# Second tap sums from superblock 10 on, and a range check of the softmax sums with a branch ahead of the last store

## The chip, the cores and the metric

The kernel runs on one core of one Trainium2 chip. A core has five engines that run side by side, each with its own instruction queue: TensorE (PE, matrix multiplications; its weight loads are shown as PEld), VectorE (DVE), ScalarE (ACT), GpSimd (POOL) and SyncE (SP, which here only issues DMAs). They wait for each other through semaphores. Matmul results go to PSUM, the small memory that only the engines reach; all other tiles are in SBUF.

The metric is the device time of one execution in microseconds. The kernel before took 746.48 us (median of three runs, 745.0 to 747.21).

## The reference

Two stages follow each other: a dynamic convolution, whose 7 weights per token and head come out of a softmax, and a two-layer network with x - tanh(x) between the layers.

```python
# x (8, 4096, 192), weight_gen (8, 4096, 8, 7), w_in (192, 2048), w_out (2048, 192)
w = weight_gen - np.max(weight_gen, axis=-1, keepdims=True)
w = np.exp(w)
w = w / (np.sum(w, axis=-1, keepdims=True) + 1e-09)
x_pad = np.concatenate([zeros (B, 6, D), x], axis=1)
x_unf = x_pad[:, idx, :].reshape(B, S, 7, 8, 24)     # idx: the token and the six before it
out = np.einsum('bshk,bskhg->bshg', w, x_unf).reshape(B * S, 192)

h = out @ w_in
g = h - np.tanh(h)
return g @ w_out
```

## The kernel before

The 32768 tokens are cut into 32 superblocks of 1024 tokens (TOK). In a superblock, partition p of 128 holds J = 8 tokens that follow each other. Superblock n goes through these steps:

- SP loads x with a halo of six tokens (`load_x`, L134, 1344 KB) and the raw weights (`load_wg`, L120).
- Softmax: ScalarE takes the exponential without subtracting the maximum (L169), VectorE sums over the 7 taps (L183), takes the reciprocal (L198) and scales (L229). The sums of a superblock lie in a tile of their own, `zsum`.
- `products`: GpSimd multiplies x by the weights of the taps, all in one expression per group of taps (L299): taps 0 and 1 (`KH` = 2), taps 2 and 3, then, in `rest`, taps 4 to 6. Taps 0 to 3 go to tile `pa` (three buffers), taps 4 to 6 to tile `pb` (one buffer). For some tokens of taps 0 and 1 VectorE does the work in GpSimd's place (`help`: a copy, L250, and a multiplication, L251). `HELP[n]` lists the places (superblock, f) at which VectorE does so for superblock n; the first entry is for token 7, the second, where there is one, for token 6, and GpSimd multiplies what is left of the 8 tokens.
- `dma_sum` (L236): a DMA that GpSimd issues adds the three taps of `pb` onto taps 0 to 2 of `pa`. It is called the first sum here (`pa<-pb`, 1152 KB). For superblocks in `TWO_SUMS` a second sum (`second_sum`, `pa<-pa`, 768 KB) adds taps 2 and 3 onto taps 0 and 1. GpSimd issues the second sum of superblock n after its first two multiplications for superblock n + 1, and it waits for the landing of the first sum.
- `conv_sums` (L384): TensorE multiplies what is left with the identity, which transposes it to channels on partitions and adds up the taps in PSUM. Where there was no second sum, four taps are left, 4 x 24 = 96 matmuls; where there was one, two taps, 48 matmuls. ScalarE copies the result to `convT` (L410).
- `gemm1` (L427): first layer, 16 column blocks f, each into one PSUM tile `ph` (three buffers, shared with the transposes). ScalarE takes the tanh (L440), VectorE subtracts (`gt`, L441).
- `out_stream` (L495): second layer, one block of 128 tokens after the other, ScalarE copies the block out (L514), and SP stores the superblock (L518).

The order of the instructions on every engine is written out by hand, in one loop over n and f. In iteration (n, f) TensorE does `gemm1(n, f)`, a share of the second layer of superblock n - 1, and at two places the transposes for superblock n + 1. A plan says where: `pairs` gives the number of second-layer pairs after each f, `t2` and `t1` the f (and the pairs ahead of it) at which the transposes of chunks 0 and 1 and of chunk 2 stand, `sums` the f of the two halves of the softmax sum of superblock n + 4, `scale` the f of its scaling. Superblocks in `DOUBLE_IN` follow plan DOUBLE, those after it STEADY:

```python
STEADY = dict(pairs=(5, 11, 0, 16, 4, 12, 6, 10, 0, 6, 10, 8, 8, 8, 8, 16), t1=(14, 8), t2=(13, 0), scale=14, sums=(1, 13))
DOUBLE = dict(pairs=(4, 12, 0, 16, 0, 16, 5, 11, 0, 5, 11, 6, 10, 0, 16, 16), t1=(15, 4), t2=(11, 4), scale=15, sums=(1, 10))
DOUBLE_IN = (4, 5, 6, 7, 8, 9, 10, 11)
```

`products(n + 2)` stands at f = 1 of iteration n, its `rest` at f = 3 (or at the last place in `HELP[n + 2]` in this iteration). SP's queue holds, for each n above 8, the load of x for n + 3, the load of weights, and then the store of n - 1, in this order. The load of x for n + 3 waits for GpSimd's first multiplication of n + 2 and for the end of the use of the buffer by n + 1.

After the loop, `gemm2_last` does the second layer of the last superblock (31), token by token j: 32 matmuls (L538), a copy on ScalarE (L551), an addition on VectorE (L552). After every second j SP stores two tokens per partition (L554).

Of the kernel before, what the change touches and what calls it, by code (L numbers as in the profile page):

```python
# [8 lines left out]
FP32 = mybir.dt.float32  # L9
BF16 = mybir.dt.bfloat16  # L10

ACT = mybir.ActivationFunctionType
AX = mybir.AxisListType


@with_exitstack
def kernel(
# [8 lines left out]
    nc = tc.nc  # L26

    B, S, D = x.shape
# [7 lines left out]
    J = 8  # L36
# [8 lines left out]
    PART = (2, 3)  # L45
    TWO_SUMS = (13, 14, 15, 16, 17, 18, 19, 20, 21, 22, 23, 24, 25, 26, 27, 28, 29, 30, 31)
    AHEAD = 4
    STORE_FIRST = 8
    EXTRA = (5, 9, 11, 13)

    HELP = {n: ((n - 2, 3),) for n in (4, 5, 6, 7, 8, 9, 10, 11, 12, 13, 14, 15, 16, 17, 18, 19, 20, 21, 22, 23, 24, 25, 26, 27, 28, 29, 30, 31)} | {9: ((7, 3), (6, 12)), 10: ((8, 3), (7, 12)), 11: ((9, 3), (8, 12)), 12: ((10, 3), (9, 12)), 13: ((11, 3), (10, 12)), 14: ((12, 3), (11, 12))}
    LAST_TAP = (4, 5, 6, 7, 8)
    X_LATE = ()
    ZERO_AT = 8
    PACE, PACED = None, ()
# [26 lines left out]
    nc.vector.memzero(zero[:])  # L82
    once = const.tile([P, 1], FP32, name="once")

    x_of = {}
# [81 lines left out]
    def softmax_exp(n):  # L167
        wg_t = wg_of.pop(n)
        last_exp[0] = nc.scalar.activation(  # L169
            out=wg_t[:].rearrange("p j h k -> p (j h k)"),  # L170
            in_=wg_t[:].rearrange("p j h k -> p (j h k)"),
            func=ACT.Exp,
        )
        e_of[n] = wg_t
# [4 lines left out]
    def softmax_sum(n, j0=0, j1=J):  # L179

        if j0 == 0:
            zsum_of[n] = wgpool.tile([P, J * H], FP32, name="zsum")
        nc.vector.reduce_sum(  # L183
            out=zsum_of[n][:, j0 * H : j1 * H],
            in_=e_of[n][:, j0:j1].rearrange("p j h k -> p (j h) k"),
            axis=AX.X,
        )

    def softmax_recip(n, j0=0, j1=J):
# [4 lines left out]
    def softmax_norm(n, bank):  # L194

        wsm = softmax_tile()
        zr_v = bank[:, 512 - J * H : 512]
        nc.vector.reciprocal(zr_v, zsum_of[n][:])  # L198

        def finish():  # L200
            scale(nc.vector, wsm[:], e_of[n], zr_v)

        wsm_of[n] = (wsm, None, None, None)
        return finish

    def softmax_norm_ramp(n, bank):
# [3 lines left out]
        zr_v = bank[:, 512 - J * H : 512]  # L210
        nc.vector.reciprocal(zr_v, zsum_of[n][:])  # L211
        if n == 2:
# [312 lines left out]
    def out_pairs(m):  # L525
        for _ in range(m):
            next(pairs)

    def gemm2_last(j, f0=0, f1=NFT):

# [21 lines left out]
        nc.vector.tensor_add(out_sb[:, j, :], po[:, 1, 0:D], ot[:])  # L552
        if j % 2 == 1:
            nc.sync.dma_start(  # L554
                out=out[n * TOK : (n + 1) * TOK, :].rearrange("(p j) e -> p j e", p=P)[
                    :, j - 1 : j + 1, :
                ],
                in_=out_sb[:, j - 1 : j + 1, :],
            )

    w_in = const.tile([P, NC, F], BF16, name="w_in")
    w_out = const.tile([P, NFT, D], BF16, name="w_out")

    ctx.enter_context(tc.manual_schedule())

# [120 lines left out]
    DOUBLE = dict(pairs=(4, 12, 0, 16, 0, 16, 5, 11, 0, 5, 11, 6, 10, 0, 16, 16), t1=(15, 4), t2=(11, 4), scale=15, sums=(1, 10))  # L686
    DOUBLE_IN = (4, 5, 6, 7, 8, 9, 10, 11)

# [18 lines left out]
    for n in range(1, NTOT):  # L707
# [5 lines left out]
        for f in range(NFT):  # L713
# [18 lines left out]
            if n == AHEAD and f == 4:  # L732
                softmax_exp(n + 4)
            if n > 1:
                for h, at in enumerate(plan["sums"]):
                    if soft and f == at:
                        softmax_sum(soft[0], h * JH, (h + 1) * JH)
# [29 lines left out]
            if f == (9 if n == 1 else 1) and n <= STORE_FIRST:  # L767
                loads(n)

    gemm2_last(0, 0, J)  # L770
    out_pairs(NFT)
    gemm2_last(0, J, NFT)
    for j in range(1, J):
        gemm2_last(j)


# [28 lines left out]
```

## Time and profile before

| | before |
|---|---|
| median of three runs | 746.48 us (745.0 to 747.21) |
| span of the profiled execution | 743.4 us |
| device time of the profiled execution itself | not told apart from the three runs |
| mean granted TensorE clock | 0.995 |
| instructions | 30037 |
| first sums (1152 KB), issue to landing, median | 28, 9.5 us |
| second sums (768 KB), issue to landing, median | 21, 7.2 us |
| stores of two tokens (192 KB) at the end | 4, 3.0 us |

The span runs from the first to the last instruction of the program; the device time has a few us around it. The page gives busy time per engine, the chain of waits that ended last, and groups of instructions by source line. A view of stretches gives, for each stretch of the span, its length, then busy time and number of instructions (x) of each engine, then the granted clock, the share of DMA time and the rate in GB/s. A timeline gives start, duration, engine, line, operation and the tiles (written<-read), then in brackets the idle time before it and what ended that. "Superblock n" as a stretch of time is iteration n of the loop, from the first tanh (L440) of it to the first of the next.

### The profile page before, as it was taken

The page shows a single profiled execution, that of the slowest core. Times are in us where ns is not written, and L with a number is a line of the kernel's source. Part 1 is how long each engine was busy: PE and PEld are TensorE (multiplying, and loading weights), DVE is VectorE, ACT ScalarE, POOL GpSimd, SP SyncE. Part 2 cuts the span into 40 slices and gives each one's busy share as a digit, 9 for nine tenths or more (in the row PEclk, how much of TensorE's full clock was granted, in tenths as well). Part 3 has the DMA queues.
Part 4 walks back from the last instruction along what each step waited for, and adds up shares of the span by engine and source line. Part 5 has one row for each costly group of instructions (what it writes and reads, how often), then busy time and mean ns, then how long its engine had stood idle before and what let it go on. Part 6 is the DMA issues. An engine that isn't in the chain of part 4 may idle for free.

```text
span 743.4 us, 30037 instructions
## 1 busy us (share of the span) xinstructions
PE 722.3 (97%) x13616; PEld 556.5 (75%) x13616; DVE 687.4 (92%) x723; ACT 638.8 (86%) x872; POOL 654.5 (88%) x163
## 2 busy tenths in 40 slices
PE   3899999999999999999999999999999999999997
PEld 2477777778777777777777777777777777877777
DVE  7999899999999999999999999999999999988893
ACT  4888888888888888989889999898998989888882
POOL 7999999999999999999999999999999999991000
PEclk9899999999999999999999999999999999999999
DMA  8925367766567668878777977877887877776112
GB/s 236 245 46 161 135 172 185 195 179 149 124 183 184 183 185 224 210 199 203 166 202 209 236 186 204 178 195 205 221 209 195 192 181 194 193 149 110 45 45 86
DMA packets 34269, 130.06 MB, mean 175 GB/s; under 512 B 4591, under 2 KB 9439, under 8 KB 30174
## 3 DMA queue, kind: packets, MB, share of 16 engines
q0 software_dynamic: 19424, 51.12, 40.4%
q1 hardware_dynamic: 14718, 77.03, 27.6%
q8 instruction: 106, 1.74, 0.9%
q14 instruction: 21, 0.17, 0.1%
HBM read 54.52 MB, written 25.17 MB: 107 GB/s over the span
## 4 chain that ended last, share of the span: by engine, by line
PE 92%; DVE 5%; ACT 1%; issue 1%; DMA 1%; SPq 0%; DVEq 0%
PE ph L427 43%; PE obank L495 43%; PE pc L384 4%; DVE gt L441 3%; PE po L538 1%; ACT th L440 1%; DVE pa L299 1%; DMA wg_t<-in_weight_gen_dram 1%; DVE zsum L183 0%; SPq L134 0%; ACT convT L402 0%; DVE obank L211 0%; DVE pa L251 0%; DVE pb L299 0%; SPq L144 0%
## 5 line engine op out<-in xcount | busy, mean ns | idle before, releaser
L441 DVE TENSOR_TENSOR gt<-ph,th 128x1024 bf16<-128x1024 f32 x512 | 601.6, 1217 | 33.4 <-ACT th L440 23.2
L440 ACT ACTIVATE th<-ph 128x1024 f32<-128x1024 f32 x512 | 512.1, 1025 | 69.2 <-PE ph L427 60.3
L427 PE MATMUL ph<-convT,w_in 64*128 64x512 bf16 x3072 | 415.1, 379 | 5.3 <-DVE gt L441 3.3
L495 PEld LDWEIGHTS <-gt 64*128 64x128 bf16 x7936 | 355.6, 94 | 80.6 <-issue 6.3
L495 PE MATMUL obank<-w_out,gt 64*128 64x192 bf16 x7936 | 408.0, 243 | 0.9 <-issue 0.8
L299 POOL TENSOR_TENSOR pa<-x_t,wsm 128x2688 bf16<-128x2688 f32 (+3 forms) x68 | 338.9, 5232 | 0.2
L299 POOL TENSOR_TENSOR pb<-x_t,wsm 128x4608 bf16<-128x4608 f32 (+2 forms) x33 | 283.8, 8601 | 0.7 <-ACT wsm L221 0.5
L427 PEld LDWEIGHTS <-w_in 64*128 64x128 bf16 x3072 | 163.0, 94 | 86.0 <-issue 18.3
L514 ACT ACTIVATE out_sb<-obank 128x192 f32<-128x192 f32 x248 | 81.3, 328 | 11.2 <-PE obank L495 10.3
L410 ACT ACTIVATE convT<-pc 128x1024 bf16<-128x1024 f32 (+1 forms) x62 | 50.1, 810 | 2.9 <-PE pc L384 2.7
L236 POOL DMA_DIRECT2D pa<-pb x28 | 36.0, 1284 | 13.7 <-POOL pb L299 9.1
L384 PEld LDWEIGHTS <-pa 64*128 64x128 bf16 x2064 | 41.5, 100 | 6.8 <-DVE pa L299 1.1
L236 POOL DMA_DIRECT2D pa<-pa x21 | 34.7, 1651 | 9.6 <-DMA pa<-pb 8.9
L384 PE MATMUL pc<-ident,pa 64*128 64x64 bf16 x1968 | 41.2, 191 | 1.8 <-POOL pa L299 0.9
L183 DVE TENSOR_REDUCE zsum<-wg_t 128x32 f32<-128x224 f32 (+1 forms) x61 | 23.6, 387 | 2.9 <-ACT wg_t L169 2.9
L169 ACT ACTIVATE wg_t<-wg_t 128x448 f32<-128x448 f32 x32 | 18.2, 570 | 6.3 <-DMA wg_t<-in_weight_gen_dram 6.2
L251 DVE TENSOR_TENSOR pa<-x_t,ph 128x384 bf16<-128x384 f32 x34 | 18.8, 554 | 2.0 <-DVE ph L250 0.3
L229 DVE TENSOR_TENSOR wsm<-wg_t,pc 128x448 f32<-128x448 f32 x27 | 16.8, 621 | 2.5
L198 DVE RECIPROCAL pc<-zsum 128x64 f32<-128x64 f32 x27 | 14.9, 550 | 0.0
L384 PE MATMUL pc<-ident,pb 64*128 64x64 bf16 x216 | 4.9, 206 | 9.0 <-POOL pb L299 9.0
L384 PEld LDWEIGHTS <-pb 64*128 64x128 bf16 x288 | 6.3, 106 | 9.5 <-POOL pb L299 9.0
L538 PE MATMUL po<-w_out,gt 64*128 64x192 bf16 x256 | 11.2, 243 | 0.0
(27 smaller groups left out, 56.8 us busy)
## 6 DMA issues: line engine op xcount, KB each, us to landing
x_t<-in_x_dram SPq DMA_DIRECT2D x31, 1344.0 KB, 7.9
pa<-pb POOLq DMA_DIRECT2D x28, 1152.0 KB, 9.5
out_dram<-out_sb SPq DMA_DIRECT2D x31, 768.0 KB, 3.9
pa<-pa POOLq DMA_DIRECT2D x21, 768.0 KB, 7.2
wg_t<-in_weight_gen_dram SPq DMA_DIRECT2D x32, 224.0 KB, 7.1
x_t<-in_x_dram SPq DMA_DIRECT2D x1, 768.0 KB
w_out<-in_moe_w_out_dram POOLq DMA_DIRECT2D x1, 768.0 KB, 9.5
out_dram<-out_sb SPq DMA_DIRECT2D x4, 192.0 KB, 3.0
```

The source lines that it names most:

```text
L183: nc.vector.reduce_sum(out=zsum_of[n][:, j0 * H : j1 * H], in_=e_of[n][:, j0:j1].rearrange("p j h k -> p (j h) k"), axis=AX.X,)
L236: return nc.gpsimd.dma_start(out=out.rearrange("p k j d -> p k (j d)"), in_=in_.rearrange("p k j d -> p k (j d)"), accum_op=mybir.AluOpTyp ...
L251: nc.vector.tensor_mul(pa[:, 0:KH, j, :].rearrange("p k (h g) -> p k h g", h=H), bass.AP(tensor=x_v.tensor, offset=x_v.offset + j * D, ap= ...
L299: return eng.tensor_mul(prod(k0, k1)[:, :, j0:j1].rearrange("p k j (h g) -> p k (j h) g", h=H), bass.AP(tensor=x_v.tensor, offset=x_v.offs ...
L384: nc.tensor.matmul(pc[r][:, col : col + R] if home else pc[:, r, col : col + R], lhsT=prods[c][gi][r * R : (r + 1) * R, 2 * j : 2 * j + 2] ...
L410: last_conv[0] = nc.scalar.activation(out=out, in_=pc[:, :, 0:cols].rearrange("p r (cj t) -> p r cj t", t=R), func=ACT.Copy,)
L427: nc.tensor.matmul(ph[:, r, :], lhsT=w_in[r * R : (r + 1) * R, c, f * P : (f + 1) * P], rhs=convT[r * R : (r + 1) * R, c, :], start=(c == ...
L440: last_act[0] = nc.scalar.activation(out=th[:], in_=ph_f, func=ACT.Tanh)
L441: last_sub[0] = nc.vector.tensor_sub(gt[:], ph_f, th[:])
L495: mm = nc.tensor.matmul(po[:, 0:D], lhsT=g_of[n][f][r * R : (r + 1) * R, col : col + P], rhs=w_out[r * R : (r + 1) * R, f, :], start=(r == ...
L514: last_act[0] = nc.scalar.activation(out=out_sb[:, j, :], in_=po[:, 0:D], func=ACT.Copy)
L538: nc.tensor.matmul(po[:, r, 0:D], lhsT=g_of[n][f][r * R : (r + 1) * R, col : col + P], rhs=w_out[r * R : (r + 1) * R, f, :], start=(f == 0 ...
```

## The change

Three things are changed.

1. `TWO_SUMS` begins at 10 and not at 13, and `DOUBLE_IN` ends at 8 and not at 11. So the superblocks 10, 11 and 12 get a second sum and 48 transposes in place of 96, and iterations 9, 10 and 11, which hold these transposes, follow plan STEADY.
2. `HELP` has a second entry for 9, 10 and 11 alone, and not for 12, 13 and 14. So VectorE's help at f = 12 of iterations 9, 10 and 11 is gone, and GpSimd multiplies seven tokens for six in taps 0 and 1 of superblocks 12, 13 and 14.
3. The softmax sums of all superblocks are kept in one tile, `zall` (128 x 2048). At f = 14 of iterations 28, 29 and 30, and after the loop, VectorE takes the largest and the smallest sum of each partition, half of the tile at a time (`sums_piece` 0 to 3). It compares them with 1e30 and 1e-18, multiplies the two answers, SP brings the 128 x 2 results into one row with a DMA, and VectorE takes the minimum: `flag`. All five engines load the flag into a register and branch. If it is 0, a loop (`general`) computes all 32 superblocks anew, with the maximum subtracted; with the inputs used here it is 1 and the branch skips this. The stores of the last superblock are cut differently: tokens 0 and 1, 2 and 3, then 4 alone ahead of the branch, and 5, 6 and 7 (288 KB) behind it.

In the order of the instructions, TensorE, VectorE, ScalarE, GpSimd and SP differ only in iterations 9 to 11 and GpSimd's matching multiplications and sums, in the pieces of the check, and behind the last additions. In the path that skips `general`, every engine but GpSimd has one or more semaphore instructions that raise its semaphores to the counts that `general` would have left; VectorE's waits for its last addition. The last store waits for that count. SP waits, in the same path, for the landing of its earlier DMAs, the one-token store among them.

```diff
-    TWO_SUMS = (13, 14, 15, 16, 17, 18, 19, 20, 21, 22, 23, 24, 25, 26, 27, 28, 29, 30, 31)
+    TWO_SUMS = (10, 11, 12, 13, 14, 15, 16, 17, 18, 19, 20, 21, 22, 23, 24, 25, 26, 27, 28, 29, 30, 31)
...
-    HELP = {n: ((n - 2, 3),) for n in (4, ..., 31)} | {9: ((7, 3), (6, 12)), 10: ((8, 3), (7, 12)), 11: ((9, 3), (8, 12)), 12: ((10, 3), (9, 12)), 13: ((11, 3), (10, 12)), 14: ((12, 3), (11, 12))}
+    HELP = {n: ((n - 2, 3),) for n in (4, ..., 31)} | {9: ((7, 3), (6, 12)), 10: ((8, 3), (7, 12)), 11: ((9, 3), (8, 12))}
...
+    STORES = {1: 0, 3: 2, 4: 4}
+    LAST_STORE = {7: 5}
+    SUM_MAX, SUM_MIN = 1e30, 1e-18
+    CHECK = {(28, 14): (0,), (29, 14): (1,), (30, 14): (2,)}
...
+    zall = const.tile([P, NTOT * J * H], FP32, name="zall")
...
-            zsum_of[n] = wgpool.tile([P, J * H], FP32, name="zsum")
+            zsum_of[n] = zall[:, n * J * H : (n + 1) * J * H]
...
+    def sums_piece(i):
+        w = NTOT * J * H // 2
+        if i < 4:
+            op = ALU.max if i < 2 else ALU.min
+            nc.vector.tensor_reduce(ends[:, i : i + 1], zall[:, i % 2 * w : (i % 2 + 1) * w], AX.X, op)
+        elif i == 4:
+            nc.vector.tensor_scalar(ends[:, 0:2], ends[:, 0:2], SUM_MAX, None, op0=ALU.is_le)
+        elif i == 5:
+            nc.vector.tensor_scalar(ends[:, 2:4], ends[:, 2:4], SUM_MIN, None, op0=ALU.is_ge)
+        elif i == 6:
+            nc.vector.tensor_mul(fine[:], ends[:, 0:2], ends[:, 2:4])
+            nc.sync.dma_start(out=fine_row[:], in_=fine[:])
+        else:
+            nc.vector.tensor_reduce(flag[:], fine_row[:], AX.X, ALU.min)
...
+    def store_last(j):
+        n = NTOT - 1
+        j0 = (STORES | LAST_STORE)[j]
+        nc.sync.dma_start(
+            out=out[n * TOK : (n + 1) * TOK, :].rearrange("(p j) e -> p j e", p=P)[:, j0 : j + 1, :],
+            in_=out_of[n][:, j0 : j + 1, :],
+        )
...
-        if j % 2 == 1:
-            nc.sync.dma_start(
...
+        if j in STORES:
+            store_last(j)
...
-    DOUBLE_IN = (4, 5, 6, 7, 8, 9, 10, 11)
+    DOUBLE_IN = (4, 5, 6, 7, 8)
...
+            for piece in CHECK.get((n, f), ()):
+                sums_piece(piece)
...
+    for piece in (3, 4, 5, 6):
+        sums_piece(piece)
     gemm2_last(0, 0, J)
     out_pairs(NFT)
     gemm2_last(0, J, NFT)
     for j in range(1, J):
+        if j == 4:
+            sums_piece(7)
         gemm2_last(j)
...
+    good = nc.values_load(flag[:], min_val=0, max_val=1)
+    with tc.If(good < 1, preferred_fallthrough_block=False):
+        with tc.For_i(0, B) as b:
+            carry = xpool.tile([P, HALO + J, D], FP32, name="x_t")
+            nc.vector.memset(carry[0:1, 0:HALO, :], 0.0)
+            with tc.For_i(0, NSB) as s:
+                general(b * NSB + s, carry)
+    store_last(J - 1)
```

## The prediction

> **What bounds the kernel now.** I read the page's busy shares and its chain first, then the busy time per stretch, cut at the first tanh (L440) of each superblock, then GpSimd's timeline, and last the end of the program.
>
> ```profile
> PE 722.3 (97%) x13616; PEld 556.5 (75%) x13616; DVE 687.4 (92%) x723; ACT 638.8 (86%) x872; POOL 654.5 (88%) x163
> ...
> q8 instruction: 106, 1.74, 0.9%
> ...
> PE 92%; DVE 5%; ACT 1%; issue 1%; DMA 1%; SPq 0%; DVEq 0%
> ```
>
> TensorE is busy almost always and holds 92% of the chain, so what is taken off TensorE shortens the span if nothing else becomes late. GpSimd is as full while it works (88% of a span of which it sits out the last tenth). The stretches below are superblocks 9, 10, 11, then 12, 14, 15, 18, then 29. Columns: length; busy time and number of instructions of PE, PEld, DVE, ACT, POOL; granted clock; DMA share; GB/s.
>
> ```profile
> 221.74:244.41 22.67, 22.67 (x454) 17.68 (x450) 21.60 (x25) 19.85 (x27) 22.37 (x6) 1.00 0.78 182
> 244.41:267.09 22.68, 22.68 (x454) 17.66 (x450) 21.59 (x25) 19.85 (x27) 22.38 (x6) 1.00 0.72 205
> 267.09:289.76 22.67, 22.67 (x454) 17.68 (x450) 21.58 (x25) 19.84 (x28) 22.37 (x7) 1.00 0.72 198
> 289.76:311.61 21.85, 21.85 (x406) 16.93 (x402) 20.93 (x24) 19.70 (x27) 21.08 (x6) 1.00 0.80 201
> 333.77:355.62 21.85, 21.85 (x406) 16.82 (x402) 21.03 (x23) 19.70 (x28) 21.09 (x6) 1.00 0.80 199
> 355.62:377.47 21.85, 21.85 (x406) 16.84 (x402) 21.03 (x23) 19.71 (x27) 21.13 (x6) 1.00 0.80 199
> 421.95:443.81 21.86, 21.86 (x406) 16.85 (x402) 21.04 (x23) 19.71 (x27) 21.40 (x6) 1.00 0.81 202
> 663.29:685.16 21.87, 21.87 (x406) 17.22 (x402) 19.50 (x19) 19.38 (x26) 9.44 (x3) 1.00 0.69 142
> ```
>
> With 96 transposes a superblock takes 22.67 us, with 48 it takes 21.85; PE is busy for all of it at full clock either way, and no other engine is.
>
> GpSimd's timeline (start, us, engine, line, operation). 216.44 is the first tap sum of superblock 10 and 217.26 the start of two multiplications for 11; 276.51 to 286.30 are the multiplications of 14 and the second sum of 13, the first there is; the last four lines are a late round.
>
> ```profile
> 216.44 1.28 POOL L236 DMA_DIRECT2D pa<-pb  x1 [0.30 <-POOL pb L299]
> 217.26 10.33 POOL L299 TENSOR_TENSOR pa<-x_t,wsm 128x2304 bf16<-128x2304 f32 x2
> 227.06 8.83 POOL L299 TENSOR_TENSOR pb<-x_t,wsm 128x4608 bf16<-128x4608 f32 x1
> ...
> 276.51 10.35 POOL L299 TENSOR_TENSOR pa<-x_t,wsm 128x2304 bf16<-128x2304 f32 x2
> 286.30 1.73 POOL L236 DMA_DIRECT2D pa<-pa  x1
> ...
> 605.19 1.28 POOL L236 DMA_DIRECT2D pa<-pb  x1 [0.30 <-POOL pb L299]
> 606.01 11.01 POOL L299 TENSOR_TENSOR pa<-x_t,wsm 128x2688 bf16<-128x2688 f32 x2
> 616.48 1.72 POOL L236 DMA_DIRECT2D pa<-pa  x1
> 626.89 1.28 POOL L236 DMA_DIRECT2D pa<-pb  x1 [0.32 <-POOL pb L299]
> ```
>
> At the end of the program VectorE is idle between the last gt and the first out_sb add, and 0.96 us before each later add.
>
> ```profile
> 725.96 2.53 DVE L441 TENSOR_TENSOR gt<-ph,th 128x1024 bf16<-128x1024 f32 x2 [0.29 <-ACT th L440]
> 730.73 0.36 DVE L552 TENSOR_TENSOR out_sb<-po,ot 128x192 f32<-128x192 f32 x1 [2.24 <-ACT ot L551]
> 739.97 0.36 DVE L552 TENSOR_TENSOR out_sb<-po,ot 128x192 f32<-128x192 f32 x1 [0.96 <-ACT ot L551]
> ```
>
> **The change, part by part. 1, TensorE in superblocks 9 to 11.** They give up 48 transposes each and take the STEADY order that 12 onward have. A stretch of exactly that kind is 21.85 us, directly behind DOUBLE ones too (289.76). So 3 x (22.67 - 21.85) = -2.46 us. As a check, groups of 64, 32 and 16 transposes last 1.11, 0.65 and 0.41 us; (1.11 + 0.65) - (0.65 + 0.41) = 0.70 of the 0.82. VectorE also loses a help pair per superblock (0.19 + 0.55 us); it was not the limit, so nothing is counted for that.
>
> **2, GpSimd: three more second sums, three multiplications of seven tokens for six.** The tokens add 10.47 - 9.79 = 0.68 us each (606.01 to 616.48 against 276.51 to 286.30); a second sum adds 0.78 to GpSimd's queue and makes the 4608-wide multiplication 9.32 in place of 8.84. All of it is GpSimd time; it costs only if TensorE gets its products late. The second sum of 10 would be issued at 217.26 + 9.79 = 227.05; the first sum has landed by then (216.44 + 9.51 = 225.95). With the 7.84 us of the one at 286.30 (7.0 to 7.8 later on) it lands at 234.9. TensorE wants the tile at the 16.24 us into superblock 9 that STEADY shows, 237.98: 3.1 us to spare. The next is issued at 227.83 + 9.6 + 0.82 + 10.47 = 248.7, lands by 256.6, and is wanted at 243.59 + 16.24 = 259.8. From there GpSimd needs 21.70 a round (605.19 to 626.89) against TensorE's 21.85, so the spare grows by 0.15 each. The cover shrinks from about 11 us to 3 but holds: 0. Behind GpSimd in SP's queue stand the x loads (released by the first multiplication of the superblock before) and, behind them, the store; with GpSimd's round for 13 starting at 260.0, x for 14 goes at 264.9, ahead of the store that follows superblock 11's start (265.4): 0.
>
> **3, range check inside the loop.** A reduction of 1024 columns: 375 ns for 224, 614 for 448, so 375 + 800 x 1.067 = 1.23 us, in superblocks 28, 29, 30 behind the gt of f = 14. There the reciprocal and scaling of earlier superblocks (0.55 + 0.62 us) are missing, and VectorE's busy time is 20.06, 19.50 and 18.94 against 21.03: 0 (bounds 0 to 0.2).
>
> **4, end of the loop.** The fourth reduction, two compares and a product on VectorE, 1.23 + 3 x 0.2 (a 128x16 copy is 190 ns) with short waits, about 2.0 us, fit between 728.49 and 730.73. SP now sends the small row of results ahead of superblock 30's store, which moves from 730.07 to about 731 and is long down by the end. The flag reduction (0.4 us) lies in the 0.96 us before the fifth add, if the row lands within 4 us; a 192 KB store takes 1.9. All 0.
>
> **5, load, branch, last store.** The last store can't be issued before VectorE has finished its last add, loaded the flag into a register, branched and raised its semaphore to the count that the skipped block would have reached. In the trace VectorE's sequencer goes on 0.02 us after the last add starts (739.99), so the load runs beside the add. No row has such a load. From below: the sequencer's semaphore rows, 0.02 to 0.06 us; then the store goes at 740.33 + 0.12 = 740.45 and not 740.36, +0.09. From above: a whole memory round trip, as the last store's own 1.87 us (740.36 to 742.23); the store goes at 739.99 + 1.87 + 0.12 = 741.98, +1.62. ACT's table load, 1.28 us, is the nearest in kind, for one register I take less, 0.8: +0.55. SP passes its own load, a wait for the landing of the one-token store (issued at 736.4, down by 738.3 to 739.5) and a jump over the skipped code before that; if the jump must fetch code, a packet of the instruction queue (q8 above: packets, MB, share of 16 engines) costs 0.9% x 16 x 743.4 / 106 = 1.0 us, which ends near 740.5 and so lies beside VectorE's path (bounds 0 to +1.0). The store itself is 288 KB for 192: (3.25 - 1.87) us per 576 KB gives +0.23 (0 to 0.5). Sum +0.78, bounds 0.1 to 3.1.
>
> The Trainium skill puts a register load at some 200 ns (Runtime: NRT & Kernel Launch, Instruction fetch mechanics) and a compare-and-branch at about 108 ns (Advanced Engine Details and Errata, Control Flow Timing). By these, an estimate, the load would hide behind the add and part 5 would be about +0.4, the time 744.4. The former page also holds that a taken branch out of the two pages in hand stalls on a fetch, which speaks for the upper bound; no row here shows either.
>
> **Sum.** -2.46 + 0.78 = -1.68: the span goes from 743.4 to 741.7. The profiled execution's own device time is not told apart; the median of the three runs, 746.48, lies 3.1 above the span, and I carry that: 744.8. One-off stalls that no engine explains (0.77 us at 378.3, 0.3 in two other superblocks) fall anew in each program: about 1 us either way.
>
> **The rivals.** *The end swallows the gain.* Load, fetch and larger store all at their upper bounds: +3.1, so 747.1, or 748 if the fetches of several engines queue. For it: no row prices the load; against: most of it runs beside other engines' end.
> *GpSimd becomes the pace* (the slower side). If its round were longer than 21.85, TensorE would lose, over the 21 superblocks that follow, 21 x the excess less the 3.1 spare; slower than before from 21 x e = 3.1 + 1.68, a round of 22.08. A round of 22.2 gives 21 x 0.35 - 3.1 = 4.2 lost, 749.1. For it: lead cut to 3 us, and a second sum waits for its first sum's landing, which took up to 11.42 us against the 11.29 there is. Against: 21.70 is measured with both sums and seven tokens.
> *The transposes were hidden anyway*, VectorE being the limit: only the tail is left, 747.3. Against: PE is busy 22.67 of 22.67.
> *A tail that costs next to nothing*, with fewer stray stalls: 743.5 to 744.1.
>
> **How the numbers follow.** This kernel's timing can't tell less than about 0.3% (2.24 us) from no change. Chances: forecast 0.60, of which 0.12 fall past -2.24 by a small tail and stray stalls; cheap tail 0.11; tail swallows 0.13, of which 0.06 past +2.24; GpSimd's pace 0.11, all slower; hidden 0.05, within. Faster 0.23, same 0.60, slower 0.17. The forecast alone spans 743.4 to 746.9; with the cheap tail and most of the swallowing one 743.0 to 748.0.
>
> **What would show it.** Right: superblocks 9 to 11 at 21.85 with 48 transposes, no PE wait for pa before L384's transposes; the last store 0.1 to 1.6 us after the last add. Wrong: PE idle ahead of the transposes from 237 us on; or a gap of over 2 us between last add and last store, or between its landing and the end.

## The result, and the profile after

The changed kernel takes 748.92 us (median of five runs, 748.66 to 749.51) against 745.67 for the kernel before (five runs, 744.72 to 747.21): a ratio of 1.0043, 95% interval 1.0032 to 1.0054. It is slower by 3.3 us; the prediction said 744.8 and a gain.

The page of the changed kernel first: the busy times, the queue that brings TensorE's code (q8: packets, MB, share of 16 DMA engines) and the chain.

```profile
PE 721.8 (97%) x13472; PEld 557.3 (75%) x13472; DVE 691.3 (93%) x725; ACT 639.0 (86%) x872; POOL 660.3 (88%) x166
...
q8 instruction: 106, 1.74, 0.9%
...
PE 73%; POOL 17%; issue 3%; DVE 2%; DMA 2%; ACT 1%; SPq 0%; POOLq 0%; DVEq 0%
```

TensorE has 144 matmuls less, as planned, and hardly any less busy time. "Issue", time in which the engine waited for nothing that the profile shows, is 3% of the chain where it was 1%. Most of that lies before 239 us, where the chain now runs through GpSimd (the 17%) up to one wait of TensorE for a second sum; from there on "issue" is 0.8% of the chain, about 4 us, where it was 0.3%. To find the place, the span is cut at the first tanh of a superblock. Stretches of the changed kernel, superblocks 9 to 11, 16 to 21, and 31 with the end (length; busy time and instructions of PE, PEld, DVE, ACT, POOL; granted clock, DMA share, GB/s):

```profile
221.79:287.83 66.04, 65.64 (x1206) 50.65 (x1202) 63.04 (x68) 59.28 (x81) 65.15 (x17) 1.00 0.87 206
...
375.61:511.70 136.09, 132.48 (x2406) 102.83 (x2402) 126.62 (x133) 118.69 (x162) 134.31 (x33) 1.00 0.80 207
...
708.95:746.90 37.95, 32.54 (x618) 27.35 (x612) 24.64 (x30) 21.04 (x33) 0.00 (x0) 0.99 0.17 66
```

The last two of them in the kernel before:

```profile
377.47:509.62 132.15, 131.52 (x2406) 101.42 (x2402) 126.36 (x133) 118.34 (x163) 128.61 (x31) 1.00 0.81 201
706.97:743.40 36.43, 32.55 (x618) 27.38 (x612) 22.21 (x25) 21.04 (x33) 0.00 (x0) 1.00 0.18 67
```

So the whole difference of the spans, 746.89 - 743.40 = +3.49, falls into three places: superblocks 9 to 11, 66.04 - 68.02 = -1.98; superblocks 16 to 21, which the change does not touch, 136.09 - 132.15 = +3.94 with the same 2406 matmuls; and the end, 37.95 - 36.43 = +1.52. The rest of the span is the same to 0.1 us.

**Superblocks 16 to 21.** What TensorE waited for in the changed kernel from 221 to 709 us (us in total, times, longest):

```profile
PE obank L521 <- issue: 2.7, 4, 1.3
PE ph L453 <- issue: 0.9, 1, 0.9
PE pc L410 <- DMA pa<-pa: 0.4, 1, 0.4
```

The kernel before has one such line here, `PE obank L495 <- issue: 0.8, 2, 0.6`. The longest of the five, in the chain of the changed kernel (start, length, what):

```profile
440.57 0.65 PE ph L453 x6
441.22 0.41 PE obank L521 x10
441.63 1.27 issue
442.90 1.08 PE obank L521 x22
443.98 0.65 PE ph L453 x6
```

TensorE stops for 1.27 us in the middle of a block of the second layer and no semaphore is named. Such stalls stand at 377.7 (0.80 us), 399.0 (0.37), 420.3 (0.27), 442.9 (1.27) and 464.8 us (0.88). The positions of the instructions at which TensorE goes on, counted over its own program, all leave the same remainder when divided by 256: 194, or 195 where a weight load stands at 194. (Where the count starts is arbitrary, so the remainder need not be 0; what counts is that it is always the same.) So each stall ends at the first instruction of a block of 256, a page: pages 53, 56, 59, 62 and 65. Both stalls of the kernel before do too (47 and 54). And the q8 line above has 106 packets of 16 KB: TensorE's 27,000 instructions make 105.5 pages. So TensorE waits for its code.

The fetch of a page begins after the page before it has begun. In the changed kernel it begins on average 2.26 us later (pages 30 to 95; 1.69 in the kernel before) and at most 4.95 (4.16). The packet then takes some 0.95 us, and TensorE goes on 1.3 to 1.5 us after its end. A page lasts 5.3 to 8.2 us, so a fetch that begins 4 to 5 us late arrives too late when the page is a short one. In all five cases 17 or 18 packets of a first sum were in flight when the page before began. Over pages 30 to 95 of the changed kernel the fetch began 3.15 us late on average where 14 or more packets of a sum were in flight at that moment (28 pages), 2.37 us late with 12 or more packets of SP's loads and stores (21 pages), and 0.10 us late with fewer than 8 of both (13 pages).

**The end.** The last additions and the last store of the changed kernel (start, length, engine, line):

```profile
741.58 0.33 ACT L585 ACTIVATE ot<-po 128x192 f32<-128x192 f32 x1 [0.99 <-PE po L572]
741.95 0.36 DVE L586 TENSOR_TENSOR out_sb<-po,ot 128x192 f32<-128x192 f32 x1 [0.96 <-ACT ot L585]
742.73 0.34 SPq L558 DMA_DIRECT2D out_dram<-out_sb  x1
```

The store goes 0.42 us after the addition's end, before 0.03. VectorE's load of the flag is a row of its own, 741.96 to 742.50, 0.54 us; the branch behind it 0.05. Landing of the store: 742.73 to 745.45 = 2.72 us against 740.36 to 742.23 = 1.87. From landing to the end of the program 1.44 against 1.17. So +0.39, +0.85 and +0.27 make the 1.5.

### The profile page after: what moved, and what is told of

It is laid out like the page before. It is cut to its first block, busy times and chain, and to the rows that moved or that the text cites. A ratio compares the mean times of both kernels' runs of the same rounds, so it can differ in the third digit from the quotient of the medians.

```text
span 746.9 us, 29794 instructions
## 1 busy us (share of the span) xinstructions
PE 721.8 (97%) x13472; PEld 557.3 (75%) x13472; DVE 691.3 (93%) x725; ACT 639.0 (86%) x872; POOL 660.3 (88%) x166
## 4 chain that ended last, share of the span: by engine, by line
PE 73%; POOL 17%; issue 3%; DVE 2%; DMA 2%; ACT 1%; SPq 0%; POOLq 0%; DVEq 0%
PE obank L521 35%; PE ph L453 34%; POOL pa L325 9%; POOL pb L325 8%; PE pc L410 3%; DMA pa<-pa 2%; PE po L572 1%; DVE gt L467 1%; DVE pa L325 1%; DMA wg_t<-in_weight_gen_dram 1%; ACT th L466 1%; POOL pa L262 0%; ACT convT L428 0%; SPq L144 0%; DVE obank L237 0%
## 5 line engine op out<-in xcount | busy, mean ns | idle before, releaser
L453 PEld LDWEIGHTS <-w_in 64*128 64x128 bf16 x3072 | 165.2, 94 | 84.8 <-issue 20.1
L262 POOL DMA_DIRECT2D pa<-pa x24 | 39.7, 1655 | 9.8 <-DMA pa<-pb 9.2
L193 DVE TENSOR_REDUCE zall<-wg_t 128x32 f32<-128x224 f32 (+1 forms) x61 | 23.7, 388 | 2.8 <-ACT wg_t L179 2.8
L277 DVE TENSOR_TENSOR pa<-x_t,ph 128x384 bf16<-128x384 f32 x31 | 17.2, 554 | 1.4
L224 DVE RECIPROCAL pc<-zall 128x64 f32<-128x64 f32 x27 | 14.9, 550 | 0.0
```

Source lines behind the costliest of these rows:

```text
L193: nc.vector.reduce_sum(out=zsum_of[n][:, j0 * H : j1 * H], in_=e_of[n][:, j0:j1].rearrange("p j h k -> p (j h) k"), axis=AX.X,)
L262: return nc.gpsimd.dma_start(out=out.rearrange("p k j d -> p k (j d)"), in_=in_.rearrange("p k j d -> p k (j d)"), accum_op=mybir.AluOpTyp ...
L453: nc.tensor.matmul(ph[:, r, :], lhsT=w_in[r * R : (r + 1) * R, c, f * P : (f + 1) * P], rhs=convT[r * R : (r + 1) * R, c, :], start=(c == ...
```

## The experiments

"Series" below means three to six neighbouring superblocks above the 21.86 us that a superblock takes from 12 on. "Lead" is the time from GpSimd's issue of a first sum to the moment at which TensorE wants that tile. Four theories stood at first: F, code pages that come late; T, the tail costs all; S, the larger program as such; G, GpSimd's sums or VectorE hold TensorE. Every kernel was compared with the kernel before on the same chip, which took 745.5 to 745.9 there.

### The range check without the new schedule

```diff
 (from the changed kernel)
-    TWO_SUMS = (10, 11, 12, 13, ...)
+    TWO_SUMS = (13, ...)
...
-    HELP ... 11: ((9, 3), (8, 12))}
+    HELP ... 11: ((9, 3), (8, 12)), 12: ((10, 3), (9, 12)), 13: ((11, 3), (10, 12)), 14: ((12, 3), (11, 12))}
...
-    DOUBLE_IN = (4, 5, 6, 7, 8)
+    DOUBLE_IN = (4, 5, 6, 7, 8, 9, 10, 11)
```

> The range check, the flag, the branch and the new cut of the last stores, with TWO_SUMS, HELP and DOUBLE_IN as before. Theory F (late code: TensorE's instructions come in pages of 256 by DMA, and while sums, x and stores fill the DMA engines a page comes late; GpSimd, no longer held by VectorE's help, keeps its DMAs in step with the pages for five superblocks): no series of stalls in superblocks 16 to 21 (132.2 us as before, not 136.1), the end from superblock 31's first tanh at 37.9 us for 36.4, so +1.5: 747.2. Rival T (the check and its branch cost all of the loss): 748.9. Rival S (the larger program moves TensorE's pages, whatever the schedule): stalls of 3 to 4 us somewhere, 749 to 751.

748.26 us (746.89 to 749.45), ratio 1.0036 [1.0023, 1.0048], a microsecond more than F had expected. The last stretch takes 38.14, +1.71. There is no series: superblocks 16 to 21 take 131.70, and two stalls, 0.66 and 0.24 us, stand at the same pages as in the kernel before, 47 and 54. So the check costs its end and no series. The other microsecond of its 2.75 is not placed: in the profiled execution 1.1 us lie ahead of superblock 16 and 0.4 in 22 to 30, while 16 to 21 are 0.45 shorter than before.

### The new schedule without the range check

The three changed lists alone (`TWO_SUMS`, `HELP`, `DOUBLE_IN`), in the kernel before.

> The kernel before with the three changed lists alone (second sums from 10, second VectorE tokens up to 11, DOUBLE up to 8), no check. F: superblocks 9 to 11 at 66.0 us for 68.0, of which one wait of 0.5 us for the second sum of 10, and stalls of TensorE without a wait in 16 to 21, +3.9; the end as before, 36.4: 747.6. T: no stalls, 743.7. S: stalls gone too, 743.7.

745.15 us, ratio 0.9992 [0.9981, 1.0004]: no difference. In the profiled execution superblocks 9 to 11 take 65.57, the full gain, and 16 to 21 take 131.15. But a series stands at 23 to 28 (22.30, 22.78, 23.58, 22.85, 21.96, 22.34):

```profile
PE obank L495 <- issue: 3.5, 6, 0.8
```

All six begin a page (75, 78, 81, 84, 87, 93). Ten of the twelve executions took 744.7 to 747.2 us, two 742.23 and 742.49; the gap fits an execution without the series, though no trace shows these two. The schedule gains what was forecast and the series takes it away; the check is not needed for it.

### 64 dummy matmuls ahead of the first transposes

```diff
+    for i in range(64):
+        nc.tensor.matmul(pad[:, i % 2, 0:R], lhsT=ident[...], rhs=ident[...], start=True, stop=True)
     conv(0, (0, 1), (2,))
```

> The changed kernel with 64 matmuls of the identity into an unused PSUM tile ahead of everything on TensorE, while it waits for the first products: 128 more instructions, so that each page boundary falls half a page earlier in the work, about 3.4 us. F: superblocks 16 to 21 no longer show 22.8, 23.0, 23.3, 22.9, 22.1, 22.0; stalls stand at other superblocks, still each at the first instruction of a page of 256; the total may fall to 745.5 or stay near 749, by where the boundaries now meet the DMAs. Rival G (GpSimd's late sums or VectorE hold TensorE in 16 to 21): the same superblocks at the same lengths within 0.1 us, 748.9.

751.35 us, ratio 1.0081 [1.0066, 1.0095]. The series moved to superblocks 12 to 16 (22.28, 24.97, 22.53, 22.45, 22.10); 16 to 21 take 131.62. TensorE from 288 to 382 us:

```profile
PE obank L521 <- issue: 3.4, 4, 1.9
PE ph L453 <- issue: 0.4, 1, 0.4
```

Each instruction of the loop now lies 128 places (64 loads and 64 matmuls) later in the program, and the stalls came at other instructions of it, again with the same remainder (pages 41, 44, 47, 50, 53). The programs of GpSimd and VectorE are unchanged, so G falls; the place follows the pages.

### The changed kernel without load, branch and general loop

```diff
-    good = nc.values_load(flag[:], min_val=0, max_val=1)
-    with tc.If(good < 1, preferred_fallthrough_block=False):
-        ...
     store_last(J - 1)
```

> The changed kernel without the load of the flag, the branch and the code behind it; the sums are still reduced, and the last store of three tokens follows directly. What is left out: the computation for sums out of range. If the end costs what the trace says: the last store is issued 0.03 us after the last addition for 0.42, and the stretch from its landing to the end is 0.95 us for 1.4, so -0.8 us; the landing itself stays at 2.7 us if it is the larger store, or falls to 1.9 if the branch beside it made it longer: 747.3 to 748.1. Superblocks 16 to 21 keep their stalls (136.1 us). Rival T: below 746.

747.93 us, ratio 1.0029 [1.0018, 1.0041]. The last stretch is 36.88: load and branch cost 37.94 - 36.88 = 1.06 us. Of the 0.45 that stay over the kernel before, 0.19 is the larger store (it lands in 2.06 us, for 1.87) and 0.26 lies behind its landing. So the store's 2.72 us in the changed kernel are mostly not its size. The queues there, from 742.7 us to the end (packets, MB, share of 16 engines):

```profile
q1 hardware_dynamic: 144, 0.29, 19.3%
q14 instruction: 3, 0.02, 1.5%
q8 instruction: 1, 0.02, 1.5%
```

The first row is the store; the other two are packets of code, one of 16 KB of TensorE's (742.92, 1.01 us) and three of 8 KB of a second code queue, two of them ahead of the landing. Without the branch the same stretch has the row of the store alone. That the code packets slow the store fits, but was not tried by itself.

Most of the loss stays, not at 16 to 21, where it was expected, but as a series at 23 to 28 (22.41, 22.99, 24.15, 22.92, 22.09, 22.44), at the pages of the schedule alone. T falls, and so does S, since the program is shorter by the whole general loop.

### The second tokens kept

```diff
 (three kernels: the changed one, the schedule alone, the changed one with
  the last store ahead of the branch)
-    HELP ... 11: ((9, 3), (8, 12))}
+    HELP ... 11: ((9, 3), (8, 12)), 12: ((10, 3), (9, 12)), 13: ((11, 3), (10, 12)), 14: ((12, 3), (11, 12))}
```

In GpSimd's timeline of the changed kernel its round is 21.69 us (367.91 to 389.60) with nothing from TensorE's side to wait for; in the kernel before it is held up by VectorE's token (`pa<-x_t,ph`, behind a gt of that superblock) and keeps in step with TensorE. Changed kernel, then the kernel before:

```profile
367.91 1.28 POOL L262 DMA_DIRECT2D pa<-pb  x1 [0.30 <-DVE gt L467]
...
389.60 1.28 POOL L262 DMA_DIRECT2D pa<-pb  x1 [0.30 <-DVE gt L467]
```

```profile
385.67 1.28 POOL L236 DMA_DIRECT2D pa<-pb  x1 [0.95 <-DVE pa L251]
```

Its lead in the kernel before is 30.7 us from superblock 14 on; in the changed one 23 to 25 at superblocks 12 to 17, and 29.6 after the series. So the next idea was to give the lead back with the tokens.

> The changed kernel with one part taken back: VectorE makes a second token of the products of superblocks 12 to 14 again, as before. Each such token shortened GpSimd's round in the kernel before (19.75 us with it, 21.64 without). Theory F (code pages of TensorE arrive late while GpSimd's sums and the x load are in flight, and the series of such stalls stands because GpSimd runs free with a lead of 22 to 24 us): GpSimd's lead, 22.8 us at superblock 11, gains 2.1 us in each of three rounds and stands at 28 to 31 from superblock 14; there is no series of four or five neighbouring superblocks above 22.5, superblocks 16 to 21 take 131.5 to 132.3 instead of 136.1, and the time is 745.0 (744.3 to 746.0). Theory L (layout luck: any change of the schedule meets such a series somewhere): a series of about 4 us at another place, time 748.3 to 749.5. Theory V (VectorE's tokens are what the change got rid of; bringing them back costs TensorE): superblocks 9 to 11 above 66.6, series unchanged, time above 749.

748.6 us, ratio 1.0041 [1.0027, 1.0056]. Theory V, more than F: superblocks 9 to 11 are back at 68.19.

```profile
PE ph L453 <- DVE pa L277: 1.6, 2, 0.8
PE obank L521 <- issue: 1.2, 3, 0.6
PE pc L410 <- DMA pa<-pa: 0.5, 1, 0.5
PE ph L453 <- issue: 0.4, 1, 0.4
```

(From 221 to 512 us.) Under plan STEADY TensorE's next block waits 0.8 us for the token, which VectorE makes in a `ph` bank. And a token beside a second sum saves GpSimd only 21.68 - 21.01 = 0.67 us, not the 1.9 that the expectation took from rows without second sums. The lead came to 27.3, not 28 to 31; the series was still there at 17 to 20, but shorter (22.65, 22.48, 22.44, 22.25; 16 to 21 at 133.58).

> The kernel before with the second sums from superblock 10 and the ordinary plan from superblock 9, but with all of VectorE's second tokens kept and without the range check. F: superblocks 9 to 11 at 65.5 to 66.1, lead at 28 to 31 from superblock 14, no series (the version without the tokens had one at 23 to 28, 3.9 us), superblocks 22 to 30 at 197.0 to 197.6; time 742.4 (741.8 to 743.5), faster than the kernel before by 2 to 3.7 us. L: 744.7 to 745.5, with a series somewhere. V: superblocks 9 to 11 above 66.6, time above 745.

746.9 us, ratio 1.0015 [1.0006, 1.0024]: the same without the check, 9 to 11 at 68.19, lead 27.0 at superblock 14, a series at 17 to 19 (23.21, 22.48, 22.44). F had expected 742.4.

> The changed kernel with the second tokens kept (as in the first of these runs) and the last store of three tokens issued ahead of the flag's load and the branch, not behind them. F with the tail as measured (load and branch 1.06 of the 1.5 us, the larger store 0.45): no series, the last stretch 36.8 to 37.1 instead of 37.94, time 744.0 (743.3 to 745.0). If the load and the branch cost their time wherever they stand, because the program's end waits for them too: last stretch 37.9, time 745.0. L: 747.5 to 748.5.

750.16 us, ratio 1.0062 [1.005, 1.0074]; last stretch 40.09, two microseconds longer than with the store behind the branch (38.12); no case had expected a longer one. SP issues the store at 742.10, at once behind the addition:

```profile
741.71 0.36 DVE L586 TENSOR_TENSOR out_sb<-po,ot 128x192 f32<-128x192 f32 x1 [0.96 <-ACT ot L585]
742.10 0.34 SPq L558 DMA_DIRECT2D out_dram<-out_sb  x1
```

But in the path around the general loop SP waits for the landing of all its stores, now of this one too: its wait passes at 746.07, its jump comes at 746.21, and only then, at 746.72, its closing row of twelve semaphore steps, 0.06 us each. Behind the branch ten of these run while the store is in flight (741.74 to 742.29 in the kernel with the tokens). Against that kernel the store goes 0.39 us earlier after the addition, lands in 3.97 us for 2.90 (+1.07), and the program ends 2.73 us after the landing for 1.44 (+1.29): the two microseconds. Why the landing is slower was not tried. So the order in the change is the better one.

### No x loads from superblock 10 on

```diff
     def load_x(n, behind=None):
+        if n >= 10:
+            x_of[n] = same_x[0]
+            return
```

> The changed kernel in which the x loads of superblocks 10 to 31 are left out and the tile of superblock 9 is used in their place (so the output from superblock 10 on is that of other data; the instructions of the engines other than the loads are the same). Theory F: from superblock 7 on the sums no longer share the DMA engines with an x load, the code pages arrive at once, and no series stands: superblocks 16 to 21 at 130.9 to 132.0, no stall of TensorE over 300 ns without a semaphore behind superblock 7, time 744.8 (744.0 to 745.8). If the x load has no part in it (the sums alone, or GpSimd's lead whatever is in flight): the series stands, at 16 to 21 or moved, time 748.3 to 749.5.

A miss for F as it stood: 748.69 us, ratio 1.0027 [1.0011, 1.0044]. Superblocks 16 to 21 take 131.15, but a series stands at 23 to 27 (22.41, 22.92, 23.88, 23.19, 22.07), from 500 to 640 us:

```profile
PE obank L526 <- issue: 4.1, 5, 1.2
```

So the series does not need the x loads. In its five stalls 16 to 19 packets of the first sum were in flight again, and some fetches began as the sum's last packets ended. Two of the ten executions took 743.74 and 744.43 us, the others 748.2 to 749.5. One thing did depend on the loads: the second sum of superblock 10, issued at 227.2, landed in 8.0 us where it took 11.3 in the changed kernel, and TensorE did not wait for it (9 to 11 at 65.58).

### An eighth of the bytes in the sums

```diff
     def dma_sum(out, in_):
+        made[0] += 1
+        js = 1 if made[0] > 12 else J
-            out=out.rearrange("p k j d -> p k (j d)"),
-            in_=in_.rearrange("p k j d -> p k (j d)"),
+            out=out[:, :, 0:js].rearrange("p k j d -> p k (j d)"),
+            in_=in_[:, :, 0:js].rearrange("p k j d -> p k (j d)"),
```

> The changed kernel in which every DMA sum of taps from the thirteenth on moves one of the eight token rows only (an eighth of the bytes in as many packets, 384 B in place of 3072), so the output is wrong from about superblock 10; GpSimd's and TensorE's instructions are the same. The run without x loads still had the series (23 to 27, 5.1 us in its profile), so x loads are not needed for it, and two of its ten executions had a time 4.5 us lower. Theory F2 (a code page of TensorE is fetched late because the sum's own packets fill the DMA engines: in the stalls so far 16 to 19 sum packets were in flight when the page before began, and the fetch began 3.4 to 5.1 us later): with the burst an eighth as large no fetch is over 3.5 us late, no stall without a semaphore over 300 ns stands behind superblock 9, GpSimd still runs free at 21.7 with a lead of 22 to 26 us, superblocks 16 to 21 take 130.9 to 131.8 and the time is 743.2 (742.3 to 744.5). If the lead or GpSimd's own work makes the stalls and not the sum's traffic: a series again, 747.5 to 749.5.

742.83 us (742.55 to 742.85, five executions), ratio 0.9961 [0.9947, 0.9975], 6.1 us below the changed kernel, check and branch included. Superblocks 9 to 11, 16 to 21, 22 to 30:

```profile
221.98:287.56 65.58, 65.58 (x1205) 50.52 (x1202) 63.05 (x68) 59.15 (x81) 64.69 (x17) 1.00 0.67 168
375.01:506.16 131.15, 131.15 (x2406) 101.08 (x2403) 126.26 (x134) 118.27 (x162) 129.37 (x31) 1.00 0.42 125
506.16:702.83 196.67, 196.67 (x3606) 151.58 (x3603) 187.35 (x189) 176.36 (x240) 165.55 (x40) 1.00 0.34 103
```

PE is busy for all of each stretch: from 221 to 709 us the view of waits has no line for TensorE. Page fetches begin 0.56 us late on average (2.26 in the changed kernel). GpSimd runs free as in the changed kernel, 21.69 us a round, its lead 22.6 at superblock 11 and 24.9 at 31, and TensorE waits for none of it. The sums' queue (packets, MB, share of 16 engines) from 300 to 500 us, changed kernel, then this one:

```profile
q0 software_dynamic: 6082, 17.78, 50.1%
```

```profile
q0 software_dynamic: 6058, 2.22, 10.4%
```

As many packets, an eighth of the bytes. F2 is confirmed: the sums' own traffic makes the code pages of the series late. It also bounds what was lost: with thin sums the changed kernel stands 2.9 us below the kernel before, check and all.

### The lists one by one

> The kernel before with the second sums from superblock 10 as the only change; VectorE's tokens and the plan for superblocks 9 to 11 stay. In the run with tokens under the ordinary plan TensorE waited 0.8 us for the token's copy (pa of VectorE) in superblocks 10 and 11, and superblocks 9 to 11 stayed at 68.19. Theory P (the plan for token superblocks takes that wait away, so the 48 transposes fewer show): superblocks 9 to 11 at 65.6 to 66.3; lead 25 to 26 us at superblock 14, five short of 30.7, so a series of 3 to 5 us follows somewhere; time 745.9 (745.0 to 747.0). Theory W (it is the tokens that cost TensorE its 0.8 us a superblock, not the transposes): 9 to 11 at 67.7 to 68.3, lead 27 at superblock 14, a series of 2 to 3 us; time 747.5 (746.5 to 748.3).

747.56 us, ratio 1.0031 [1.0021, 1.0041], nearest to W, for another reason. Superblocks 9 to 11 take 69.69; under the old plan TensorE wants the second sum of 10 two microseconds before it lands (221 to 300 us):

```profile
PE pc L384 <- DMA pa<-pa: 2.0, 1, 2.0
PE ph L427 <- DVE gt L441: 0.6, 2, 0.3
PE pc L384 <- issue: 0.4, 1, 0.4
```

> The kernel before with the tokens of superblocks 12 to 14 and the plan of 9 to 11 cut as the only change; second sums stay at 13 and later. If the 48 transposes cost TensorE 0.82 us a superblock: 9 to 11 at 67.7 to 68.3. If the tokens and their plan do: 65.6 to 66.3. GpSimd's rounds 10 to 12 without token and without second sum, from 19.75 and the 0.68 us that a token saved in the runs with tokens: 20.4; lead at superblock 13 26 to 28 us, three to five short of 30.7, so theory F2 has a series of 2 to 4 us. Time 747.5 in the first case (746.5 to 749.0), 745.5 in the second (744.0 to 747.0).

747.12 us, ratio 1.0021 [1.0011, 1.003]; 9 to 11 at 69.67. Superblocks 9 and 10 take 22.45 each, where neither of the two cases had put them, and 11 takes 24.78 with two page stalls (1.0 and 0.94 us). The lead is 30.7 from superblock 13 on, and no series follows. From the schedule alone this run differs only in `TWO_SUMS`, so a superblock without and with the second sum can be compared, both free of waits (this run's superblock 9, then that of the schedule alone):

```profile
222.07:244.52 22.45, 22.45 (x454) 17.62 (x450) 21.20 (x24) 19.89 (x28) 22.15 (x6) 1.00 0.78 183
223.03:244.89 21.86, 21.86 (x406) 16.83 (x402) 20.96 (x24) 19.71 (x28) 21.56 (x7) 1.00 0.89 209
```

The 48 transposes are worth 0.59 us of the 0.82 there; the other 0.22 went with plan and tokens.

> The kernel before with the second sums from superblock 10, and VectorE's second tokens and the plan for them extended to the products of superblock 20 (superblocks 9 to 17), so that GpSimd's lead is earned by its own shorter rounds (21.0 us) and not by stalls of TensorE. Theory P: TensorE at 21.86 in 9 to 17, lead 30 by superblock 20, no series or one below 2 us; time 743.3 (742.3 to 745.0), faster than before. Theory W: superblocks 9 to 17 at 22.6 to 22.7 each, lead 30 already by superblock 15, no series; time 749.5 (748.5 to 750.5).

750.07 us, ratio 1.0053 [1.0036, 1.0069], near W: 22.44 in superblocks 12 to 17, of which 0.29 is a wait of TensorE for a gt behind the token, 2.7 us of waiting for the second sum of 10, and no series. VectorE's tokens cost TensorE about as much as they give GpSimd. The second sums alone and the cut of tokens and plan alone both lose in 9 to 11; only together do they bring it to 65.6.

## Why the prediction was wrong, point by point

**1, TensorE in 9 to 11: right, but for a wait.** -2.46 was forecast; the schedule alone measured 65.57 - 68.02 = -2.45, the changed kernel -1.98. The price of the plan as a whole was right. The prediction gave most of it to the 48 transposes (0.70 of 0.82 by its check) and nothing to VectorE's tokens; the run with the cut of tokens and plan gives the transposes 0.59, and plan and tokens the rest.

**2, GpSimd: the landing was mis-sized.** The working gave the second sum of 10 the 7.84 us of a row at 286.30, so 3.1 us to spare. It was issued at 227.13, as said (227.05), landed after 11.34 us, and TensorE waited 0.4; superblock 9 took 22.33. The row taken had an x load ahead of it too, issued at 281.31, but the superblock's store came only behind it, at 292.55. Here both stood ahead:

```profile
222.13 0.33 SPq L144 DMA_DIRECT2D x_t<-in_x_dram  x1
222.51 1.40 SPq L130 DMA_DIRECT2D wg_t<-in_weight_gen_dram  x1
224.59 0.34 SPq L544 DMA_DIRECT2D out_dram<-out_sb  x1
```

Without the x load, and with the store ahead, it lands in 8.0. So it is load and store together that took the 3.1 us. The round, 21.70, was right.

**3 and 4, the check inside the loop and at its end: 0, as said.** The reductions take 1.21 us (1.23 forecast); superblocks 28 and 30 are unchanged, 29 is 0.26 longer (not so with thin sums, 21.87 as before, so it is not the reduction's own time), and the last addition ends 33.36 us into superblock 31 in both kernels.

**5, load, branch, last store: +0.78 forecast, +1.52 measured,** inside its bounds of 0.1 to 3.1. The flag's load was over-priced (0.8; it takes 0.54 on VectorE, the store goes 0.39 later for 0.55). The size of the store was priced right: +0.23 forecast, +0.19 in the run without the branch. What was missed is that the same store lands another 0.66 later with the branch (2.72 for 2.06): the prediction put the fetch of code beside VectorE's path, but it ran beside the store. The 0.27 behind the landing were not in the sum either; they stand without the branch too (0.26). The Trainium skill (Runtime: NRT & Kernel Launch, Instruction fetch mechanics) has some 200 ns for a register load (there from HBM); the rows here, from SBUF, show 0.47 to 0.54 us, and the measurement decides.

**The stalls: the step that failed.** The prediction saw them ("One-off stalls that no engine explains (0.77 us at 378.3, 0.3 in two other superblocks) fall anew in each program: about 1 us either way") and took them for chance. They have a cause, late code pages, and the change feeds it: +3.94 in superblocks 16 to 21, more than everything else in the sum. The span was to be 741.7 and is 746.9; of the 5.2 us between them the stalls are 3.9, the end 0.7 and the wait for the second sum 0.5. By the medians of the single parts the schedule alone gained 0.4 instead of 2.5, so in most executions the series took about 2 us of it, and the check alone cost 2.75. The view of waits of the kernel before named both of its stalls, and their places, at 329.2 and 378.3 us, could have been counted in the program: a page boundary each time. At the second of them 13 packets of SP's loads and stores were in flight and none of a sum.

The Trainium skill (Runtime: NRT & Kernel Launch, Instruction fetch mechanics) has the page too, blocks of 16 KB or 256 instructions that the engine's own DMA queue brings in while the current block runs, and holds the fetch to be mostly hidden. The first half agrees with every stall here; the second does not hold beside a full set of DMA engines, with TensorE stopped up to 1.9 us (the kernel with the dummy matmuls).

Why a series and not single stalls, is argued from the numbers and was not tried by itself. A superblock has 800 instructions of TensorE (400 matmuls with a weight load each); three pages, 768, take 768 / 800 x 21.86 = 21.0 us, GpSimd's free round 21.68. So a third page on begins 0.7 us earlier against the sums' burst, unless TensorE stands still for as much. The five stalls of the series are 0.72 us long on average, and TensorE goes on after them at intervals of 21.8 us on average: the stalls hold TensorE in step with the burst. In the kernel before GpSimd waits for TensorE in most rounds (21.85 to 22.4 us from superblock 14 to 25): a stall of TensorE moves the burst with it, the boundary drifts on, and single stalls remain. The change set GpSimd free with a lead of 23 us. In the run with thin sums the same free GpSimd makes no series, because its burst is short. The series end when the lead has come to 28 to 30 us; in the changed kernel GpSimd still runs free then (rounds of 21.68 at superblocks 22 and 23), and what ends a series is open, as is why it stands at 16 to 21 in one kernel and at 23 to 28 in another with the same pages.

**The time around the span.** The prediction carried 3.1 us, the median of the runs less the span of one execution. Where one execution lists both it is 1.8 in the changed kernel (748.66 and 746.9). The profiled execution was faster than the median; the term was 1.3 too large, and hid part of the miss.

**The rivals.** GpSimd as the pace, the slower side, hit the time (749.1) by the wrong mechanism: its round is 21.68 and TensorE waited 0.4 us in all for a sum. The end that swallows the gain happened in part, 1.5 of its 3.1. A tail that costs next to nothing did not come. The transposes were not hidden.

Of what would show it wrong, "PE idle ahead of the transposes from 237 us on" came true, 0.4 us at 238.6. The stalls of the series stand in no row of that list.

## What to carry to other kernels

Idle time of a busy engine under "issue" should be placed in the engine's program before it is called chance: count to the instruction, and see whether it begins a block of 256. Where it does, the engine waited for its code, here beside the kernel's own DMAs, and an edit that shifts a DMA burst against a long unrolled loop can cost more than it saves; take the burst's bytes away once, as an experiment, to learn how much is at stake. Price a DMA's landing from a row that has the same other transfers ahead of it and beside it.

## What the runs showed of the hardware

- TensorE's code comes in packets of 16 KB, 106 in this program, some 0.95 us each. Where the sums were thin, the fetch of a page began 0.56 us after the start of the page before, on average; at the stalls it began 2.6 to 5.2 us after it, and TensorE resumed 1.2 to 1.6 us after the packet's end. In 13 traces all 52 stalls of over 0.23 us that no semaphore explains, from superblock 9 to 30, begin a page; at 48 of them 16 to 19 packets of a sum were in flight when the page before began. At the other four it was 13 to 16 packets of SP's loads and stores, at one of them together with the last of a sum. So other transfers than the sums seem to do it too; only the sums were taken away.
- A program with a spread of several microseconds can owe it to this: 744.7 to 747.2 and 742.2 to 742.5 for one kernel, 742.55 to 742.85 once the sums were thin.
- A load of one register from SBUF takes 0.47 to 0.54 us on all five engines, a compare-and-branch 0.04 to 0.10, TensorE's second one 0.19 to 0.41.
- A second sum of 768 KB landed in 7.8 us with an x load issued ahead of it (the row at 286.30), in 8.0 with a store, and in 11.3 with both; one row each.
- A store issued ahead of the skipped loop instead of behind it cost 2 us: it landed 1.07 us slower, and SP's jump and closing semaphore steps came only after the landing.
